# A retention layer and a rational FFN on one core: every engine in a hand-written order, two chunks landed in FFN buffers, weights joined in two VectorE steps

## The chip, the core and the metric

The kernel runs on one NeuronCore of a Trainium2 chip. The core has a matrix engine (TensorE, PE in the profile, with its weight loads as PEld), three engines for elementwise work (VectorE or DVE, ScalarE or ACT, GpSimd or POOL), and an engine that issues DMAs (SyncE or SP). Each takes its own instructions in the order in which they stand in its queue; semaphores make one wait for another. The metric is the device time of one execution in microseconds.

## The reference

A retention layer (a linear attention with a decaying state) feeds a feed-forward layer with a rational activation:

```python
for t in range(S):          # B, H, S, D = 4, 8, 768, 64
    state = gamma[None, :, None, None] * state + np.einsum('bhd,bhe->bhde', k[:, :, t], v[:, :, t])
    y[:, :, t] = scale * np.einsum('bhd,bhde->bhe', q[:, :, t], state)
...
h = x @ w_in                # x: 3072 tokens x 512, w_in: 512 x 2048
P = a[0] + a[1] * h + a[2] * h2 + a[3] * h3
Q = 1.0 + np.abs(b[0]) * np.abs(h) + np.abs(b[1]) * h2
g = P / (Q + 1e-06)
return (g @ w_out).astype(np.float32)   # w_out: 2048 x 512
```

The weights arrive as 64-bit floats and are made into 32-bit ones on the chip.

## The kernel before

**Attention.** The 3072 tokens are 24 chunks of 128, six to a batch element. A chunk has four tiles of 256 KB (`kT`, `qT`, `v`, `k`; the last chunk of a batch element needs no `k`). Its work comes in two parts. Part 0: POOL scales `v` and the state, PE makes the scores `pa` (16 small matmuls), VectorE multiplies them with the causal mask into `aT`. Part 1: PE adds into `px` what the state recalls (L213), the values (L221) and the new outer product of `k` and `v` (L233); VectorE scales the result, ScalarE rounds it to `xh`, VectorE takes the rest `xl`, and adds the outer product to the state.

**FFN.** Four chunks make a block of 512 tokens, six blocks `n`; the hidden layer is 16 tiles `f` of 128. One pair `(n, f)` is a slot: `gemm_in` (12 matmuls into `ph`: high and low parts of `x` and of the weights), then `poly` and `ratio` on ScalarE, VectorE and POOL, `split` of the result into `gh` and `gl`, and three slots later (`LAG`) `gemm_out`, 12 matmuls into the four accumulators `po`. `order` lists the 96 slots: blocks 0 and 1 with the first half of the hidden tiles, then both with the second half (slots 0 to 31, so that weights are needed half as fast), then blocks 2 to 5 whole. The halves of blocks 0 and 1 are parked in DRAM and added later.

**Weights.** Each of 32 weight tiles lands as `raw` (512 KB, pairs of 32-bit words). To decode one, ScalarE takes the magnitude of the high word into a PSUM bank `u`; VectorE shifts it (L106), joins the low word's top bits (L109) and the sign (L115) into `t`; ScalarE rounds `t` to the high half of `w` (L125), POOL takes the rest (L126).

**Memory.** Of PSUM's eight banks four hold `po` (and, before `po` exists, `u` and `px`), and four are one pool for `u`, `px`, `pa` and `ph`. Chunks have two buffers of each kind.

**Order.** Only SP's queue stands as the code has it. For the other four engines a scheduler with a timeline of its own decides the order; source order only sets which buffers are reused. Chunks 0 to 3 run ahead of slot 0, chunks 4 to 7 are placed in slots 0 to 7, chunks 8 to 11 in slots 24 to 31, and each later block's chunks in the 16 slots ahead of it.

Of the kernel before, what the change touches and what calls it, by code (L numbers as in the profile page):

```python
# [19 lines left out]
def tile_retention_rational_ffn(  # L20
# [31 lines left out]
    ps = ctx.enter_context(tc.tile_pool(name="ps", bufs=8 - SPB, space=PSUM))  # L52
# [4 lines left out]
    def bank(name, dtype=F32):  # L57

        if name in ("u", "px") and not o_tiles:
# [12 lines left out]
    qcon = const.tile([P, 1], F32, name="qcon")  # L72
    state = const.tile([P, NP, D], F32, name="state")
# [19 lines left out]
    def decode():  # L93

        ts = {}

        def magnitude(i):


            ts[i] = u = bank("u", U32)  # L100
            nc.scalar.activation(  # L101
                u.bitcast(F32), raws[i][:, :, 1].bitcast(F32), AF.Abs, scale=2.0 ** -112
            )

        def shift(i):
            nc.vector.tensor_scalar(ts[i], ts[i], 3, None, ALU.logical_shift_left)  # L106

        def low(i):
            nc.vector.scalar_tensor_tensor(  # L109
                ts[i], raws[i][:, :, 0], 29, ts[i], ALU.logical_shift_right, ALU.bitwise_or  # L110
            )

        def sign(i):
            t = ff.tile([P, DM], U32, name="t", bufs=TBUFS)
            nc.vector.scalar_tensor_tensor(  # L115
                t, raws[i][:, :, 1], 0x80000000, ts[i], ALU.bitwise_and, ALU.bitwise_or
            )
# [12 lines left out]
        for i in range(len(tiles)):  # L130
            if i + 1 < len(tiles):
                magnitude(i + 1)
            low(i)
            if i + 1 < len(tiles):
                shift(i + 1)
            sign(i)
            split_weight(i)
            done.add(tiles[i])
            yield

    decoding = decode()

    def need(m, f):
        while (m, f) not in done:
            next(decoding)
# [205 lines left out]
    def attend(k):  # L351
        for i, part in parts.get(k, ()):
# [7 lines left out]
            if k < 0:  # L360
                fetch()
# [109 lines left out]
```

## Time and profile before

| | |
|---|---|
| time, median of 3 runs | 664.7 us (664.12 to 664.72) |
| the profiled execution | 666.62 us, span of its instructions 664.8 us |
| granted TensorE clock, mean | 0.98 |
| PE idle before its last matmul | 31.5 us (span 664.8, busy 628.4, 4.9 behind the last matmul) |
| DMA landings, median | `raw` 6.3 and 7.0 us, `kT` 2.7 us, `v` 3.1 us |
| bytes moved | 52.36 MB, 43.33 MB read from HBM |

The page of the profile gives each engine's busy time, its share in 40 slices of the span, and groups of instructions of one line and shape with their mean time and with what ended the idle time before them (`<-` names it). A table of stretches gives busy times between two moments. In a timeline row stand start, length, engine, line, operation, what is written `<-` what is read, a count, and in brackets the idle time before and what ended it. PE's instructions are pipelined, so a busy PE can still be slow: how far it is from its best rate is seen from counts.

### The profile page before, as it was taken

Reading aid. Unit: us, or ns where it says so; the run is one execution under the profiler, and the core shown is the slowest. Engines: PE = TensorE matmul, PEld = TensorE weight load, DVE = VectorE, ACT = ScalarE, POOL = GpSimd, SP = SyncE. Lnnn points to the kernel's source line nnn. Section 1 sums busy time; section 2 is a strip of 40 time slices with the busy share of each in tenths; the row PEclk is TensorE's granted clock in tenths of the full one; section 3 lists DMA queues with packets and bytes.
Section 4 is the critical chain, followed back from the end, with each engine's and each line's share of the span. In section 5 each row is a group of like instructions: output and inputs, shape, how many; then the busy total and the mean of one; then the engine's idle time right before and its main releaser. Section 6 shows DMA issues by size and latency. Waiting matters only on the chain.

```text
span 664.8 us, 9995 instructions
## 1 busy us (share of the span) xinstructions
PE 628.4 (95%) x3712; PEld 508.6 (76%) x3712; DVE 457.4 (69%) x749; ACT 426.8 (64%) x715; POOL 323.9 (49%) x272
## 2 busy tenths in 40 slices
PE   4657999899999999999999999999999999999997
PEld 3545787688788778878888878888888888888885
DVE  4967879898876866684566657566656756766663
ACT  3436668898884555664676566666566566777773
POOL 3645457576654434443544434544444344454442
PEclk9677999999999999999999999999999999999999
DMA  8878434100102332340110222111221000010001
GB/s 306 325 230 347 160 115 170 64 0 1 64 1 80 111 128 80 103 120 17 48 49 0 65 87 74 33 24 41 65 80 33 1 0 1 12 52 1 0 1 63
DMA packets 24384, 52.36 MB, mean 79 GB/s; under 512 B 3088, under 2 KB 3216, under 8 KB 24336
## 3 DMA queue, kind: packets, MB, share of 16 engines
q1 hardware_dynamic: 24336, 51.73, 22.9%
q8 instruction: 29, 0.48, 0.3%
q14 instruction: 19, 0.16, 0.1%
HBM read 43.33 MB, written 8.39 MB: 78 GB/s over the span
## 4 chain that ended last, share of the span: by engine, by line
PE 86%; DVE 5%; DMA 3%; ACT 2%; issue 2%; POOL 1%; SPq 0%; ACTq 0%; POOLq 0%; DVEq 0%
PE po L305 39%; PE ph L259 37%; PE pa L197 4%; PE px L221 3%; PE px L213 2%; PE px L233 1%; DMA raw<-in_w_out 1%; DMA raw<-in_w_in 1%; POOL w L126 1%; DVE t L115 1%; DMA k<-in_k 1%; DVE u L109 1%; DVE ph L283 1%; DVE q L282 0%; ACT u L101 0%
## 5 line engine op out<-in xcount | busy, mean ns | idle before, releaser
L259 PE MATMUL ph<-xh,w 128*128 128x512 f32 x768 | 206.7, 393 | 4.2 <-ACT xh L243 2.2
L305 PE MATMUL po<-w,gh 128*128 128x512 f32 x768 | 201.8, 396 | 2.5 <-ACT t L322 2.5
L272 POOL TENSOR_TENSOR q<-q,s 128x512 f32<-128x512 f32 x96 | 124.2, 1294 | 144.6 <-ACT s L271 143.0
L291 POOL TENSOR_TENSOR gl<-p,gh 128x512 fp32r<-128x512 f32 x96 | 123.7, 1293 | 116.7 <-ACT gh L290 61.8
L259 PEld LDWEIGHTS ph<-xh,w 128*128 128x128 f32 x768 | 144.4, 189 | 36.5 <-DVE p L284 2.8
L305 PEld LDWEIGHTS po<-w,gh 128*128 128x128 f32 x768 | 141.0, 188 | 35.5 <-ACT t L322 3.3
L274 DVE TENSOR_TENSOR p<-ph,p 128x512 f32<-128x512 f32 x96 | 66.1, 689 | 103.2 <-ACT p L273 103.2
L305 PE MATMUL po<-w,gl 128*128 128x512 f32 x384 | 109.5, 390 | 0.0
L290 ACT CAST gh<-p 128x512 fp32r<-128x512 f32 x96 | 59.5, 620 | 69.8 <-DVE p L284 65.6
L282 DVE SCALAR_TENSOR_TENSOR q<-q,qcon,ph 128x512 f32<-128x512 f32 x96 | 71.4, 744 | 47.6 <-ACT ph L281 46.9
L259 PE MATMUL ph<-xl,w 128*128 128x512 f32 x384 | 104.2, 392 | 0.0
L270 ACT ACTIVATE q<-ph 128x512 f32<-128x512 f32 x96 | 57.2, 596 | 69.4 <-PE ph L259 68.9
L280 ACT ACTIVATE s<-q,qcon 128x512 f32<-128x512 f32 x96 | 69.6, 725 | 42.1 <-POOL q L272 41.3
L259 PEld LDWEIGHTS ph<-xl,w 128*128 128x128 f32 x384 | 72.6, 189 | 15.4
L305 PEld LDWEIGHTS po<-w,gl 128*128 128x128 f32 x384 | 72.0, 188 | 15.2
L271 ACT ACTIVATE s<-q,babs 128x512 f32<-128x512 f32 x96 | 78.0, 812 | 0.0
L273 ACT ACTIVATE p<-ph,par_sb 128x512 f32<-128x512 f32 x96 | 74.3, 774 | 0.0
L275 DVE SCALAR_TENSOR_TENSOR p<-p,par_sb,ph 128x512 f32<-128x512 f32 x96 | 71.4, 744 | 1.8
L283 DVE SCALAR_TENSOR_TENSOR ph<-p,par_sb,ph 128x512 f32<-128x512 f32 x96 | 72.0, 750 | 0.0
L284 DVE SCALAR_TENSOR_TENSOR p<-q,ph 128x512 f32<-128x512 f32 x96 | 64.7, 683 | 1.3
L281 ACT ACTIVATE ph<-s 128x512 f32<-128x512 f32 x96 | 57.9, 603 | 4.6 <-DVE p L275 2.3
L126 POOL TENSOR_TENSOR w<-t,w 128x512 fp32r<-128x512 f32 x32 | 41.1, 1286 | 23.6 <-ACT w L125 23.4
(31 smaller groups left out, 439.4 us busy)
## 6 DMA issues: line engine op xcount, KB each, us to landing
raw<-in_w_in SPq DMA_DIRECT2D x16, 512.0 KB, 6.3
raw<-in_w_out SPq DMA_DIRECT2D x16, 512.0 KB, 7.0
kT<-in_kT SPq DMA_DIRECT2D x24, 256.0 KB, 2.7
qT<-in_qT SPq DMA_DIRECT2D x24, 256.0 KB, 2.9
v<-in_v SPq DMA_DIRECT2D x24, 256.0 KB, 3.1
k<-in_k SPq DMA_DIRECT2D x20, 256.0 KB, 3.5
out<-t SPq DMA_DIRECT2D x16, 256.0 KB, 2.4
half<-t SPq DMA_DIRECT2D x8, 256.0 KB, 2.3
```

Of the source, the lines that this page charges most:

```text
L259: nc.tensor.matmul(ph, w1[f][:, part, kt * P : (kt + 1) * P], x[:, kt], start=(i == 0), stop=(i == 3 * NP - 1),)
L271: nc.scalar.activation(s, q, AF.Identity, bias=babs[:, 0:1], scale=babs[:, 1:2])
L272: nc.gpsimd.tensor_mul(q, q, s)
L273: nc.scalar.activation(p, ph, AF.Identity, bias=par_sb[:, 2:3], scale=par_sb[:, 3:4])
L274: nc.vector.tensor_mul(p, ph, p)
L275: nc.vector.scalar_tensor_tensor(p, p, par_sb[:, 1:2], ph, ALU.add, ALU.mult)
L280: nc.scalar.activation(s, q, AF.Abs_reciprocal_sqrt, bias=qcon[:, 0:1])
L282: nc.vector.scalar_tensor_tensor(q, q, qcon[:, 0:1], ph, ALU.add, ALU.mult)
L283: nc.vector.scalar_tensor_tensor(ph, p, par_sb[:, 0:1], ph, ALU.add, ALU.mult)
L284: nc.vector.scalar_tensor_tensor(p, q, 2.0, ph, ALU.subtract, ALU.mult, reverse0=True)
L291: nc.gpsimd.tensor_sub(gl, p, gh.bitcast(F32))
L305: nc.tensor.matmul(o_tiles[n][tt], g_[:, tt * P : (tt + 1) * P], w2[f][:, part], start=(first and m == 0), stop=(last and m == 2),)
```

## The change

Four things change together.

1. **Order.** All four compute engines are scheduled by hand: their instructions stand in source order. The old parts of attention and decode become small functions, and `opening()` and `run()` call them in an order written out. The opening goes chunk by chunk with one weight tile decoded in each; every slot decodes one more until all are done. Values come behind the outer product and the recall; `gh` of a slot is made in the next one.
2. **Landings.** `kT`, `qT`, `k` and `v` of chunks 2 and 3 land in buffers of the FFN (`gh`, `gl`, `q`) which are not yet in use, so that six chunks are loaded ahead.
3. **Decode.** ScalarE reads the fourth byte of each low word and writes its top three bits (scale 1/32, a bias, rounding) to `t`; VectorE's first step shifts the magnitude and joins these bits, the second joins the sign. The shift as a step of its own is gone. The weights are decoded four hidden tiles of `w_in` ahead instead of two, in two halves.
4. **FFN.** In the slots that decode but have no part of attention (8 to 23), the step `s` runs on POOL as a tensor_scalar instead of on ScalarE. `ph` gets two banks of its own, and `u`, `px`, `pa` share the other two. Copies of `po` alternate between ScalarE and VectorE, and parked halves are fetched a slot ahead.

```diff
-    ps = ctx.enter_context(tc.tile_pool(name="ps", bufs=8 - SPB, space=PSUM))
+    ps = ctx.enter_context(tc.tile_pool(name="ps", bufs=(8 - SPB) // 2, space=PSUM))
...
-        return ps.tile([P, TB], dtype, name=name, tag="bank")
+        return ps.tile([P, TB], dtype, name=name, tag="ph" if name == "ph" else "bank")
...
-        def shift(i):
-            nc.vector.tensor_scalar(ts[i], ts[i], 3, None, ALU.logical_shift_left)
-        def low(i):
-            nc.vector.scalar_tensor_tensor(
-                ts[i], raws[i][:, :, 0], 29, ts[i], ALU.logical_shift_right, ALU.bitwise_or
-            )
...
+    def decode_low(i):
...
+        ts[i] = ff.tile([P, DM], U32, name="t", bufs=3)
+        byte = raws[i].rearrange("p m w -> p (m w)").bitcast(U8)[:, 3::8]
+        nc.scalar.activation(ts[i], byte, AF.Identity, bias=lcon[:, 0:1], scale=1.0 / 32)
...
+    def decode_join(i):
...
+        nc.vector.scalar_tensor_tensor(
+            u, u, 3, ts[i], ALU.logical_shift_left, ALU.bitwise_or
+        )
+        nc.vector.scalar_tensor_tensor(
+            ts[i], raws[i][:, :, 1], 0x80000000, u, ALU.bitwise_and, ALU.bitwise_or
+        )
...
+    borrowed = {2: ("gh", "gh", "q", "gl"), 3: ("gh", "gl", "q", "gl")}
...
+    def opening():
+
+        scale_v(0)
+        scores(0)
+        for i in range(SPB):
+            mask(i)
+            outer(i)
+            recall(i)
+            values(i)
+            if i == 0:
+                decode_read(0)
+            update(i)
+            decode_join(i)
+            prepare(i + 1)
+            if i + 1 < SPB:
+                scores(i + 1)
+            x_out(i)
+            decode_split(i)
+            decode_rest(i)
+            decode_read(i + 1)
+        decode_join(SPB)
+        decode_read(SPB + 1)
...
+        if on_pool:
+            nc.gpsimd.tensor_scalar(
+                s, q, babs[:, 1:2], babs[:, 0:1], op0=ALU.mult, op1=ALU.add
+            )
+        else:
+            nc.scalar.activation(s, q, AF.Identity, bias=babs[:, 0:1], scale=babs[:, 1:2])
...
     def run():
...
+            plain = part is None and tile_ < len(tiles)
...
+                mid[k] = poly_scalar(gemm_in(*order[k]), plain)
...
+            if 0 < k <= nslot:
+                g[k - 1] = split(mid.pop(k - 1)[1])
...
+            if part == 1:
+                outer(chunk)
+                recall(chunk)
+                values(chunk)
             if k >= LAG:
                 n, f = order[k - LAG]
                 gemm_out(n, f, *g.pop(k - LAG))
...
+            if part == 0:
+                scores(chunk)
+                load_k_t(chunk + 2)
+            if plain:
+                decode_read(tile_ + 1)
+                decode_join(tile_)
+            if k < nslot:
+                ratio_scalar(*mid[k])
...
+            elif k < nslot:
+                ratio_vector(*mid[k])
```

The number of matmuls on PE doesn't change, nor that of the DMAs. Three places show what the new order does.

VectorE from its first step in the opening, before the change (L106, L109, L115 are the three steps of decode, L202 the mask, L242 and L244 the two halves of `x`, L247 the state):

```order
L106 TENSOR_SCALAR u<-u 128x512
L109 SCALAR_TENSOR_TENSOR u<-raw,u 128x512
L202 TENSOR_TENSOR aT<-pa,causal_sb 128x512
L115 SCALAR_TENSOR_TENSOR t<-raw,u 128x512
L202 TENSOR_TENSOR aT<-pa,causal_sb 128x512
L242 TENSOR_TENSOR px<-px,xdec_sb 128x256
L106 TENSOR_SCALAR u<-u 128x512
L244 TENSOR_TENSOR xl<-px,xh 128x2x128
L109 SCALAR_TENSOR_TENSOR u<-raw,u 128x512
L115 SCALAR_TENSOR_TENSOR t<-raw,u 128x512
L242 TENSOR_TENSOR px<-px,xdec_sb 128x256
L244 TENSOR_TENSOR xl<-px,xh 128x2x128
```

Chunk 0 stood between the steps of two weight tiles, and four more tiles were joined before chunk 2. Now its whole step reads so (L222 the mask, L269 the state, L126 and L129 the two joins, L281 and L286 the halves of `x`), and the next chunk's mask follows:

```order
L222 TENSOR_TENSOR aT<-pa,causal_sb 128x512 x2
L269 COPY state<-px 128x256
L126 SCALAR_TENSOR_TENSOR u<-u,t 128x512
L129 SCALAR_TENSOR_TENSOR t<-raw,u 128x512
L281 TENSOR_TENSOR px<-px,xdec_sb 128x256 x2
L286 TENSOR_TENSOR xl<-px,xh 128x2x128 x2
L222 TENSOR_TENSOR aT<-pa,causal_sb 128x512 x2
```

The state's update moved ahead of `x`, and one tile is decoded to a chunk.

PE where `gemm_out` sets in, before the change (L259 is `gemm_in`, L305 `gemm_out`, L197 scores, L221 values):

```order
L221 MATMUL px<-aT,v 64x128 x8
L259 MATMUL ph<-xh,w 128x512 x4
L259 MATMUL ph<-xl,w 128x512 x4
L259 MATMUL ph<-xh,w 128x512 x4
L197 MATMUL pa<-qT,kT 128x128 x4
L305 MATMUL po<-w,gh 128x512 x4
L305 MATMUL po<-w,gl 128x512 x2
L197 MATMUL pa<-qT,kT 128x128 x4
L305 MATMUL po<-w,gh 128x512 x2
L305 MATMUL po<-w,gl 128x512
```

And the same kind of place now, slots 4 and 5 (L325 `gemm_in`, L380 `gemm_out`, L213 scores, L234 outer product, L258 values):

```order
L380 MATMUL po<-w,gh 128x512 x8
L380 MATMUL po<-w,gl 128x512 x4
L213 MATMUL pa<-qT,kT 128x128 x8
L325 MATMUL ph<-xh,w 128x512 x4
L325 MATMUL ph<-xl,w 128x512 x4
L325 MATMUL ph<-xh,w 128x512 x4
L234 MATMUL px<-v,k 64x64 x8
L258 MATMUL px<-aT,v 64x128 x8
L380 MATMUL po<-w,gh 128x512 x8
L380 MATMUL po<-w,gl 128x512 x4
```

Scores stood in the middle of a `gemm_out`; now each kind of work stands in one piece, and each part of a chunk in a slot of its own.

ScalarE in a slot that decodes without attention, before the change (L270, L271 and L273 are abs, `s` and `p`, L280 and L281 rsqrt and square, L290 `gh`, L101 and L125 decode):

```order
L290 CAST gh<-p 128x512
L270 ACTIVATE q<-ph 128x512
L273 ACTIVATE p<-ph,par_sb 128x512
L280 ACTIVATE s<-q,qcon 128x512
L271 ACTIVATE s<-q,babs 128x512
L281 ACTIVATE ph<-s 128x512
L101 ACTIVATE u<-raw 128x512
L125 CAST w<-t 128x512
```

The rsqrt there belongs to the slot before. Now, in slot 9 (L336 and L344 abs and `p`, L364 `gh` of the slot before, L110 and L118 the two reads of decode, L353 and L354 rsqrt and square, L139 the rounding of `w`):

```order
L336 ACTIVATE q<-ph 128x512
L344 ACTIVATE p<-ph,par_sb 128x512
L364 CAST gh<-p 128x512
L110 ACTIVATE t<-raw,lcon 128x512
L118 ACTIVATE u<-raw 128x512
L353 ACTIVATE s<-q,qcon 128x512
L354 ACTIVATE ph<-s 128x512
L139 CAST w<-t 128x512
```

`s` is gone to POOL, a second read has come, and rsqrt and square of a slot stand in that slot, behind `gh` of the one before.

More of the change, by code (lines that the diff above doesn't have):

```diff
@@ L10 @@
 U32 = mybir.dt.uint32
+U8 = mybir.dt.uint8
 AF = mybir.ActivationFunctionType
@@ L57, in bank @@
     def bank(name, dtype=F32):
-        if name in ("u", "px") and not o_tiles:
+        if name in early:
             early[name] += 1
@@ L141, in tile_retention_rational_ffn, with decode_read, decode_high @@
[L141 to L145, printed above, removed]
+    us, ts = {}, {}
+    def decode_read(i):
+        decode_low(i)
+        decode_high(i)
+    def decode_low(i):
+        if i >= len(tiles):
+            return
+        ts[i] = ff.tile([P, DM], U32, name="t", bufs=3)
+        byte = raws[i].rearrange("p m w -> p (m w)").bitcast(U8)[:, 3::8]
+        nc.scalar.activation(ts[i], byte, AF.Identity, bias=lcon[:, 0:1], scale=1.0 / 32)
+    def decode_high(i):
+        if i >= len(tiles):
+            return
+        us[i] = bank("u", U32)
+        nc.scalar.activation(
+            us[i].bitcast(F32), raws[i][:, :, 1].bitcast(F32), AF.Abs, scale=2.0 ** -112
+        )
@@ new lines, in prepare, with scores @@
+    def prepare(i):
+        if i < NSTEP:
+            scale_state(i)
+            scale_v(i)
+    def scores(i):
+        st = steps[i]
+        pa = [bank("pa").rearrange("p (h t) -> p h t", t=P) for _ in range(2)]
+        for aj in range(NP):
+            for r in range(2):
+                rows = slice(r * D, (r + 1) * D)
+                nc.tensor.matmul(
+                    pa[r][:, aj], st["kT"][rows, aj], st["qT"][rows, aj], start=True, stop=True
+                )
+        st["pa"] = pa
@@ L194, in attention, with mask, outer @@
+    def mask(i):
+        st = steps[i]
+        for r in range(2):
+            st["aT", r] = at.tile([P, NP, P], F32, name="aT")
+            nc.vector.tensor_mul(
+                st["aT", r], st["pa"][r], causal_sb.unsqueeze(1).broadcast_to([P, NP, P])
+            )
+    def outer(i):
+        st = steps[i]
+        px = st["px"] = [bank("px") for _ in range(2)]
+        if i % C < C - 1:
+            pk = st["pk"] = px[1][:, TB // 2 :].rearrange("p (h d) -> p h d", d=D)
             for aj in range(NP):
@@ new lines, in values @@
+    def values(i):
+        st, c = steps[i], i % C
+        for r in range(2):
+            for a in range(2):
+                for j in range(2):
+                    nc.tensor.matmul(
+                        st["px"][r][j * D : (j + 1) * D, a * P : (a + 1) * P],
+                        st["v"][:, 4 * a + 2 * r + j],
+                        st["aT", r][:, 2 * a + j],
+                        start=(c == 0),
+                        stop=(c == 0 or a == 1), skip_group_check=True,
+                    )
@@ L338, in tile_retention_rational_ffn @@
     }
-    parts = {-1: [(i, part) for i in range(SPB) for part in range(2)]}
+    parts = {}
     for n in range(1, NB):
```

349 lines of the change are left out of this document (180 added, 169 removed).

## The prediction

> **What bounds the kernel now.** I read the busy times first, then the slices of the span, then a table of stretches of the instructions that touch a decoded weight tile `w`, and last the timeline of the opening. TensorE (PE) is the bound, and where it isn't busy the time is lost:
>
> ```profile
> PE 628.4 (95%) x3712; PEld 508.6 (76%) x3712; DVE 457.4 (69%) x749; ACT 426.8 (64%) x715; POOL 323.9 (49%) x272
> PE   4657999899999999999999999999999999999997
> PEclk9677999999999999999999999999999999999999
> ```
>
> After the fourth slice (16.6 us each) PE is nearly full. But "busy" doesn't say whether the stage moves at its best rate. The FFN has 2304 large matmuls (96 slots, 12 of `ph` and 12 of `po` each), and the best rate is in the chain, late in the kernel:
>
> ```profile
> 635.43 2.72 PE ph L259 x12
> ```
>
> 2.72 us for 12 is 0.2267 us each: 5.44 us a slot, 522 us in all. The stretches below are cut where slots 0, 7, 24, 48, 64 and 80 start and where the last matmul ends; PE's count in them is of large matmuls alone:
>
> ```profile
> core 0: us, PE busy (x) PEld busy (x) ACT busy (x) POOL busy (x), PEclk, DMA share, GB/s
> 0.00:43.02 43.02, 0.00 (x0) 0.00 (x0) 6.80 (x11) 12.96 (x11) 0.80 0.80 286
> 43.02:102.42 59.40, 41.12 (x156) 30.31 (x157) 3.72 (x6) 8.75 (x7) 0.94 0.63 220
> 102.42:195.28 92.86, 88.39 (x385) 71.70 (x384) 9.26 (x15) 19.41 (x15) 1.00 0.12 46
> 195.28:360.23 164.95, 137.21 (x577) 106.41 (x576) 0.00 (x0) 0.00 (x0) 1.00 0.24 74
> 360.23:462.08 101.85, 89.74 (x385) 71.38 (x384) 0.00 (x0) 0.00 (x0) 1.00 0.17 53
> 462.08:564.54 102.46, 89.76 (x385) 71.38 (x384) 0.00 (x0) 0.00 (x0) 1.00 0.09 29
> 564.54:659.90 95.36, 95.36 (x421) 78.64 (x419) 0.00 (x0) 0.00 (x0) 1.00 0.03 12
> ```
>
> So: 43.0 us pass before the first large matmul, and at 102.4 us, with all of chunks 0 to 7 of attention done, only 156 of the 2304 are through. The third stretch holds 384 (87.1 us at the best rate; a count one higher is one that straddles a cut) and takes 92.9: 5.8 lost. The next three hold 576 + 384 + 384 and 16 chunks; above the best rate they take 34.4 + 14.8 + 15.4 = 64.6 us, 4.0 a chunk, but 3.7 in the best of them. The last holds 420 at the best rate. Behind 659.9 lie 4.9 us of copies and stores.
>
> Why the first stretch is long shows in PE's timeline:
>
> ```profile
> 4.21 2.08 PE L197 MATMUL pa<-qT,kT 64*128 64x128 f32 x16 [4.21 <-DMA qT<-in_qT]
> ...
> 25.54 2.08 PE L197 MATMUL pa<-qT,kT 64*128 64x128 f32 x16 [3.55 <-DMA qT<-in_qT]
> ...
> 37.96 1.23 PE L213 MATMUL px<-qT,state 64*64 64x128 f32 x16 [6.56 <-POOL state L190]
> ...
> 60.36 2.07 PE L259 MATMUL ph<-xh,w 128*128 128x512 f32 x4
> 62.23 1.91 PE L259 MATMUL ph<-xl,w 128*128 128x512 f32 x4
> 63.94 1.74 PE L259 MATMUL ph<-xh,w 128*128 128x512 f32 x4
> ```
>
> Chunk 3's scores wait for a landing at 25.5, and its recall for the state until 38.0. VectorE had been joining weights that nobody needed yet (the order's first rows show it). The last three rows are one `ph` of 12 at 60.4: 5.25 us instead of 2.72.
>
> **The change, part by part.** These are the group rows for the steps that move, with mean ns and what they waited for:
>
> ```profile
> L290 ACT CAST gh<-p 128x512 fp32r<-128x512 f32 x96 | 59.5, 620 | 69.8 <-DVE p L284 65.6
> L280 ACT ACTIVATE s<-q,qcon 128x512 f32<-128x512 f32 x96 | 69.6, 725 | 42.1 <-POOL q L272 41.3
> L271 ACT ACTIVATE s<-q,babs 128x512 f32<-128x512 f32 x96 | 78.0, 812 | 0.0
> L281 ACT ACTIVATE ph<-s 128x512 f32<-128x512 f32 x96 | 57.9, 603 | 4.6 <-DVE p L275 2.3
> L282 DVE SCALAR_TENSOR_TENSOR q<-q,qcon,ph 128x512 f32<-128x512 f32 x96 | 71.4, 744 | 47.6 <-ACT ph L281 46.9
> L283 DVE SCALAR_TENSOR_TENSOR ph<-p,par_sb,ph 128x512 f32<-128x512 f32 x96 | 72.0, 750 | 0.0
> L284 DVE SCALAR_TENSOR_TENSOR p<-q,ph 128x512 f32<-128x512 f32 x96 | 64.7, 683 | 1.3
> L202 DVE TENSOR_TENSOR aT<-pa,causal_sb 128x512 f32<-128x512 f32 x48 | 31.6, 684 | 9.8 <-PE pa L197 9.8
> L106 DVE TENSOR_SCALAR u<-u 128x512 uint32<-128x512 uint32 x32 | 22.2, 695 | 13.5 <-ACT u L101 13.3
> L109 DVE SCALAR_TENSOR_TENSOR u<-raw,u 128x512 uint32<-128x512 uint32 x32 | 22.1, 692 | 0.4
> L101 ACT ACTIVATE u<-raw 128x512 f32<-128x512 f32 x32 | 20.4, 637 | 12.5 <-DMA raw<-in_w_in 8.0 <-DMA raw<-in_w_out 3.2 <-DVE t L115 1.0
> L242 DVE TENSOR_TENSOR px<-px,xdec_sb 128x256 f32<-128x256 f32 x48 | 20.3, 426 | 8.6 <-PE px L221 8.2 <-PE px L233 0.3
> L272 POOL TENSOR_TENSOR q<-q,s 128x512 f32<-128x512 f32 x96 | 124.2, 1294 | 144.6 <-ACT s L271 143.0
> ```
>
> *Opening (landings, decode, order).* In the new order VectorE does in each of the four steps: two masks (1.37 us), the state's update (0.42, as one of the 256-wide rows), two joins (1.38), two 256-wide products and two subtractions (4 x 0.43 = 1.7). That is 4.9 us, with no wait but for PE's values, which the update and joins cover, and for ScalarE's `xh` between products and subtractions. The bound from landings: chunks 0 to 3 (four 256 KB tiles each), the four `raw` tiles of 512 KB queued through chunk 3 and 0.33 MB of constants are 6.6 MB, 23 us at the table's 286 GB/s; reading tile 3 (two ScalarE steps), joining it and making chunk 3's `x` is about 4 us more. From the first scores' end (4.21 + 2.08 = 6.3) four steps of 5 us give 26.3. I take **27 us** for the first large matmul, where it was 43.0; ends 25 and 33 (a landing lost at each of chunks 2 and 3, priced near the 3.55 wait). On SP's queue the loads of chunks 4 and 5 now stand ahead of the later `raw` tiles and wait for the buffers of chunks 0 and 1; these come free in the first two steps, by 17 us, while what is queued ahead of them takes 23 us to land, so nobody waits for that.
>
> *Slots 0 to 7.* The same 156 matmuls and chunks 4 to 7 took 59.4 us before, which would end at 86.4. Step by step: the first `ph` runs like the one at 60.4, 5.25 us, until 32; slot 0 then runs abs, s, p, two products, mask, read, two joins and three ratio steps to 41; slots 1 and 2 add 6 and 8 (mask and join sit in front of the even slots' ratio, and ScalarE's read waits for the mask to free a bank, with the next slot's abs queued behind it; PE's second `ph` bank covers that); at 55 PE has done four `ph`, one `po` and six chunks. Left are 8 x 2.72 and two chunks at 3.7, 29.2 us: 84.2, and a stall of 1. I take **85 us** where 102.4 stood: **17.4 gained**. VectorE's sum over eight slots (five ratio and poly steps 3.6, a join pair 1.4, mask or `x` 1.9: 6.9, or 55 in all) gives 82; each slot paying 1.5 us of handovers more gives 95.
>
> The Trainium skill's "TensorE: Matmul & The Clock Gate", Part 1, has PE drop to half rate after an idle window of about 3.4 us and stay there for as long. The rows at 60.4 agree: 5.25 for 2.72, after an idle stretch. By that rule alone slots 1 and 2 could be cold too, 5 us on PE and, with nothing to cover it, 90 for 85; I count one.
>
> *Slots 8 to 23 (a tile decoded in each).* The third join step goes: 32 x 0.695 = 22 us less on VectorE. ScalarE gets a read of one byte per weight; its price is not in the trace. The nearest rows are the plain read at 637 (which strides over words as well) and the activation with a bias tile at 812: I take 0.70, ends 0.60 and 0.81. Sixteen of the `s` steps move from ScalarE to POOL: 812 ns go, and a POOL step comes that the trace doesn't have; nearest is L272's 1294 (two inputs, one operation), which I take, with ends 1.04 and 2.59 (twice that row, for two operations). POOL then has four steps of 1.29, 5.2 of 5.44 us.
>
> The Trainium skill's "GPSIMD Engine Reference" (§3 and §4.1) speaks against this move: elementwise work belongs on VectorE. It gives one-input work some 1.8 cycles an element, 769 ns for 512, which no row here shows; by that the POOL step would be an estimated 0.8 us and the sum below the same, since POOL isn't last.
>
> What is last is a loop through ScalarE and VectorE: `gh` of the slot before, the two reads, rsqrt, square, three ratio steps, which release the next `gh`: 0.62 + 0.70 + 0.64 + 0.73 + 0.60 + 0.74 + 0.75 + 0.68 = 5.46. Four neighbours of it don't depend on each other and overlap by 0.1, as the first pair of rows here does (0.60 long, next start 0.49 later); some five handovers add about 0.2:
>
> ```profile
> 605.55 0.60 ACT L270 ACTIVATE q<-ph 128x512 f32<-128x512 f32 x1 [0.70 <-PE ph L259]
> ...
> 606.04 0.78 ACT L273 ACTIVATE p<-ph,par_sb 128x512 f32<-128x512 f32 x1
> ...
> 611.84 0.69 DVE L284 SCALAR_TENSOR_TENSOR p<-q,ph 128x512 f32<-128x512 f32 x1
> ```
>
> So 5.3 against 5.44: PE sets the pace, barely. Copies of `po` halves are shared by two engines and come a slot ahead of need. I put **2.0 lost** for the 5.8 of before (ends 0.5 and 16): **3.8 gained**.
>
> *Two banks for `ph`.* `ph` of slot k+2 waits for the ratio of slot k. From the start of abs, right behind `ph`, to the end of the ratio the three rows above show 611.84 + 0.69 - 605.55 = 7.0; PE has 3 x 2.72 = 8.16 us to do in between, more with attention. No cost; without that cover it costs half the excess in every slot.
>
> *Chunks 8 to 23.* PE's rows alternate in whole blocks instead of single matmuls. I take 3.6 each, 58 us for 64.6: **6.6 gained**; ends 55 and 65. The tail keeps its 4.9.
>
> Sum: 17.4 + 3.8 + 6.6 = 27.8. The profiled execution has a span of 664.8 in a time of 666.6; the median of the runs is 664.7, and I subtract from that: **637 us**.
>
> **Rivals.**
> - *The loop or POOL paces slots 8 to 23.* With the POOL step at 2.59, POOL needs 6.5 a slot, 16 us in sixteen; with the loop at 6.0, 9 us: 645 to 653. For it: ScalarE's and VectorE's sums are within 0.2 of PE's. Against: L272's idle, 144.6 us.
> - *The first tensor_scalar on POOL comes late.* POOL has run only products and subtractions. A delay of d at slot 8 costs d less the 1.2 of slack, once. "GPSIMD Engine Reference", §2.1, gives some 6 us for a first call into freshly loaded code. From rows alone the price lies between 0 and a slot, 5.4: up to 642. Against: the order shows no extra load.
> - *Chunks 2 and 3 don't land sooner.* Then the opening keeps its waits of 3.55 and 6.56: 27 becomes 37, 647.
> - *Slower: the fixed order makes a chain of every slot.* Before, a scheduler filled each wait; now each engine stops at the first wait in its queue, and two `ph` banks give PE two slots of cover. Where the chain from `ph` to ratio is longer than 8.8 us, PE loses over 0.33 in each of 88 slots, 29 us, and the kernel ends above 666. Against: the late rows show 7.0, and the new order puts `s` ahead of `p`.
> - *Better:* slot 7 ends at 82, nothing lost to 23, chunks at 3.5: 630.
>
> **How the numbers follow.** Forecast 0.55; the loop or POOL 0.17; better 0.10; late landings 0.08; late first call 0.05; slower chain 0.05. The range 630 to 650 holds the forecast, the late call and landings, most of the better case and half of the paced one: above eight in ten. A run can tell about 0.2% (1.3 us) from no change. Faster 0.94, same 0.01, slower 0.05.
>
> **What would show it.** First `ph` near 27 us and the `ph` that follows 60 `po` near 85; slots 8 to 23 at 5.44 with POOL's `s` at 1.0 to 1.3; a chunk at 3.6 to 3.7 with no wait of PE on a ratio. A first `ph` after 33, a wait of PE's `ph` on the last ratio step in most slots, or a POOL step over 1.6 makes the prediction wrong.

## The result, and the profile after

| | before | after |
|---|---|---|
| time, median of 4 runs | 664.71 us (664.12 to 664.97) | 648.58 us (647.85 to 649.76) |
| ratio | | 0.976 (95%: 0.9743 to 0.9777) |
| span of the profiled execution | 664.8 us | 648.0 us |

The forecast was 637 us in a range of 630 to 650. Sign and range hold, but 16.1 us were gained where 27.8 were forecast. The three lines of the page that were read first, after the change:

```profile
PE 623.6 (96%) x3712; PEld 503.8 (78%) x3712; DVE 460.5 (71%) x730; ACT 441.7 (68%) x721; POOL 333.6 (51%) x288
PE   5777999999999999999999999999999999999997
PEclk9877999999999999999999999999999999999999
```

PE is full from the fifth slice on, as before, but slices 2 to 4 stand at 7. The table of stretches, cut at the same slots as before (0, 8, 24, 48, 64, 80, and the last matmul's end), of instructions that touch a decoded `w`:

```profile
0.00:34.51 34.51, 0.00 (x0) 0.00 (x0) 1.86 (x3) 3.86 (x3) 0.89 0.97 359
34.51:97.99 63.48, 42.99 (x156) 31.86 (x156) 6.59 (x11) 13.53 (x11) 0.87 0.57 195
97.99:185.62 87.63, 87.63 (x385) 72.05 (x385) 9.69 (x16) 20.04 (x16) 1.00 0.15 56
185.62:346.08 160.46, 135.91 (x577) 106.74 (x576) 1.22 (x2) 3.90 (x3) 1.00 0.25 76
346.08:446.88 100.80, 89.41 (x385) 71.46 (x384) 0.00 (x0) 0.00 (x0) 1.00 0.17 53
446.88:548.42 101.54, 89.40 (x385) 71.46 (x384) 0.00 (x0) 0.00 (x0) 1.00 0.09 29
548.42:644.27 95.85, 95.67 (x421) 78.56 (x419) 0.00 (x0) 0.00 (x0) 1.00 0.04 14
```

The columns are those of the table before: stretch and length, then busy time and count of PE, PEld, ACT and POOL, the granted clock, DMA share and GB/s. Term by term, with 0.2267 us for a large matmul as the best rate:

| | before | forecast | after | gained (forecast) |
|---|---|---|---|---|
| first `ph` | 43.0 | 27 | 34.5 | 8.5 (16.0) |
| slots 0 to 7 | 59.4 | 58 | 63.5 | -4.1 (1.4) |
| lost in slots 8 to 23 | 5.8 | 2.0 | 87.63 - 87.06 = 0.6 | 5.2 (3.8) |
| chunks 8 to 23 | 64.6 | 58 | 29.9 + 13.7 + 14.5 = 58.1 | 6.5 (6.6) |
| slots 80 to 95 over the best rate | 0.1 | 0.1 | 0.6 | -0.5 (0) |
| behind the last matmul | 4.9 | 4.9 | 3.7 | 1.2 (0) |

The gains add up to 16.8, the difference of the two spans. Everything from slot 8 on came out within 1.5 us of its term or better. The first 98 us brought 4.4 of the 17.4 us that they were to bring.

**Where the opening's time went.** PE's timeline, chunks 2 and 3 (L213 scores, L234 outer product, L247 recall, L258 values):

```profile
21.98 0.69 PE L234 MATMUL px<-v,k 128*64 128x64 f32 x16 [1.81 <-DMA qT<-in_qT]
22.60 0.67 PE L247 MATMUL px<-qT,state 64*64 64x128 f32 x16
23.19 1.86 PE L258 MATMUL px<-aT,v 128*64 128x128 f32 x16
24.98 2.00 PE L213 MATMUL pa<-qT,kT 64*128 64x128 f32 x16
28.77 0.69 PE L234 MATMUL px<-v,k 128*64 128x64 f32 x16 [1.79 <-DVE xl L286]
```

And VectorE's in the same step (L271 update, L126 and L129 joins, L281 products, L286 subtractions, L222 masks):

```profile
25.16 0.42 DVE L271 TENSOR_TENSOR state<-px,state 128x256 f32<-128x256 f32 x1 [2.24 <-PE px L258]
25.50 0.69 DVE L126 SCALAR_TENSOR_TENSOR u<-u,t 128x512 uint32<-128x512 uint32 x1
26.23 0.69 DVE L129 SCALAR_TENSOR_TENSOR t<-raw,u 128x512 uint32<-128x512 uint32 x1
26.83 0.76 DVE L281 TENSOR_TENSOR px<-px,xdec_sb 128x256 f32<-128x256 f32 x2
27.75 0.76 DVE L286 TENSOR_TENSOR xl<-px,xh 128x256 fp32r<-128x256 f32 x2 [0.16 <-ACT xh L282]
28.42 1.28 DVE L222 TENSOR_TENSOR aT<-pa,causal_sb 128x512 f32<-128x512 f32 x2
```

One step is a closed loop. From outer product to outer product it takes 28.77 - 21.98 = 6.79 us: 1.21 until the values start (23.19), 1.97 until the update starts (25.16), 0.34 + 1.33 for update and joins (26.83), 0.92 for products and rounding (27.75), 1.02 until `xl` has left the two `px` banks (28.77). (In the row at 21.98 the profile names a landing of `qT`, which the outer product doesn't read; `xl` left the banks at 20.97 + 0.76 = 21.73, and the outer products of chunks 1 and 3 come as shortly behind their `xl`.) VectorE's part of the loop is 6.79 - 2.24 = 4.55, with 0.16 of waiting for `xh` in it, under the forecast's 4.9; the rest is 2.24 of waiting at the update. The update reads only the outer product, finished by 22.7, but that lies in the same tile as part of the values, and the profile has the update start when the *values* end. Behind it in VectorE's queue stand two joins that need neither. The forecast had the joins cover the wait for the values; they stand behind the instruction that waits.

**Where slots 0 to 7 lost 5.5 us.** PE's rows in slots 0, 2 and 3 (L325 `gemm_in`, L380 `gemm_out`):

```profile
34.52 2.07 PE L325 MATMUL ph<-xh,w 128*128 128x512 f32 x4 [2.72 <-ACT xh L282]
...
49.27 1.20 PE L325 MATMUL ph<-xh,w 128*128 128x512 f32 x4 [2.74 <-DVE p L359]
50.30 1.59 PE L325 MATMUL ph<-xl,w 128*128 128x512 f32 x4
51.69 1.91 PE L325 MATMUL ph<-xh,w 128*128 128x512 f32 x4
...
60.17 0.40 PE L247 MATMUL px<-qT,state 64*64 64x128 f32 x2 [2.25 <-DVE aT L222]
62.29 1.12 PE L247 MATMUL px<-qT,state 64*64 64x128 f32 x14 [1.71 <-DVE t L129]
63.34 1.97 PE L258 MATMUL px<-aT,v 128*64 128x128 f32 x16
65.25 1.22 PE L380 MATMUL po<-w,gh 128*128 128x512 f32 x2
```

In slot 3 PE has done its fourth `ph` by 57.9 and then stands at the recall of chunk 5, first for the mask, then for a bank that `u` of a weight tile holds until the join L129 ends (62.2). Queued behind it is the first `gemm_out`, whose `gl` had been ready since 51.3. Slot 4 starts at 69.26, 34.7 us after slot 0, where the forecast's steps put it 28 after; slots 4 to 7 then take 28.7, forecast 30.

### The profile page after: what moved, and what is told of

Read it like the earlier page. It is cut to its first block, busy times and chain, and to the rows that moved or that the text cites. A ratio compares the mean times of both kernels' runs of the same rounds, so it can differ in the third digit from the quotient of the medians.

```text
span 648.0 us, 9942 instructions
## 1 busy us (share of the span) xinstructions
PE 623.6 (96%) x3712; PEld 503.8 (78%) x3712; DVE 460.5 (71%) x730; ACT 441.7 (68%) x721; POOL 333.6 (51%) x288
## 4 chain that ended last, share of the span: by engine, by line
PE 88%; ACT 3%; DVE 3%; DMA 3%; issue 1%; SPq 1%; POOLq 0%; DVEq 0%; ACTq 0%
PE ph L325 40%; PE po L380 39%; PE px L258 3%; PE pa L213 3%; PE px L247 2%; PE px L234 2%; DMA qT<-in_qT 1%; DMA k<-in_k 1%; DMA xdec_sb<-in_xdec 1%; ACT s L342 1%; DVE u L126 1%; ACT q L336 0%; SPq L174 0%; DVE t L129 0%; DVE p L348 0%
## 5 line engine op out<-in xcount | busy, mean ns | idle before, releaser
L325 PE MATMUL ph<-xh,w 128*128 128x512 f32 x768 | 211.2, 397 | 5.8 <-DVE p L359 2.9
L380 PE MATMUL po<-w,gh 128*128 128x512 f32 x768 | 201.0, 394 | 0.0
L325 PEld LDWEIGHTS ph<-xh,w 128*128 128x128 f32 x768 | 143.8, 190 | 39.4 <-ACT xh L282 4.1
L380 PEld LDWEIGHTS po<-w,gh 128*128 128x128 f32 x768 | 143.3, 189 | 32.7 <-ACT p L344 1.9
L336 ACT ACTIVATE q<-ph 128x512 f32<-128x512 f32 x96 | 57.2, 596 | 126.4 <-PE ph L325 126.3
L380 PE MATMUL po<-w,gl 128*128 128x512 f32 x384 | 110.9, 390 | 0.2 <-POOL gl L365 0.2
L325 PE MATMUL ph<-xl,w 128*128 128x512 f32 x384 | 104.2, 394 | 0.0
L357 DVE SCALAR_TENSOR_TENSOR q<-q,qcon,ph 128x512 f32<-128x512 f32 x96 | 71.4, 744 | 39.3 <-ACT ph L354 39.2
L325 PEld LDWEIGHTS ph<-xl,w 128*128 128x128 f32 x384 | 72.8, 190 | 15.8
L380 PEld LDWEIGHTS po<-w,gl 128*128 128x128 f32 x384 | 72.4, 188 | 15.6 <-POOL gl L365 0.6
L353 ACT ACTIVATE s<-q,qcon 128x512 f32<-128x512 f32 x96 | 69.3, 722 | 15.3 <-POOL q L343 15.3
L344 ACT ACTIVATE p<-ph,par_sb 128x512 f32<-128x512 f32 x96 | 73.1, 761 | 0.0
L364 ACT CAST gh<-p 128x512 fp32r<-128x512 f32 x96 | 58.8, 612 | 15.1 <-DVE p L359 15.1
L342 ACT ACTIVATE s<-q,babs 128x512 f32<-128x512 f32 x80 | 65.3, 817 | 2.7
L354 ACT ACTIVATE ph<-s 128x512 f32<-128x512 f32 x96 | 57.8, 602 | 10.2 <-DVE p L349 0.4
```

The costliest lines, as they stand in the source:

```text
L325: nc.tensor.matmul(ph, w1[f][:, part, kt * P : (kt + 1) * P], x[:, kt], start=(i == 0), stop=(i == 3 * NP - 1),)
L342: nc.scalar.activation(s, q, AF.Identity, bias=babs[:, 0:1], scale=babs[:, 1:2])
L344: nc.scalar.activation(p, ph, AF.Identity, bias=par_sb[:, 2:3], scale=par_sb[:, 3:4])
L353: nc.scalar.activation(s, q, AF.Abs_reciprocal_sqrt, bias=qcon[:, 0:1])
L357: nc.vector.scalar_tensor_tensor(q, q, qcon[:, 0:1], ph, ALU.add, ALU.mult)
L380: nc.tensor.matmul(o_tiles[n][tt], g_[:, tt * P : (tt + 1) * P], w2[f][:, part], start=(first and m == 0), stop=(last and m == 2),)
```

## The experiments

"After" is the changed kernel at 648.58 us; each experiment was timed beside the kernel before. Times are medians of four runs (of six for e10); the last two columns, and the stretches in the text, are from one profiled execution each.

| | edit | us | ratio to before (95%) | first `ph` | slot 8 starts |
|---|---|---|---|---|---|
| after | | 648.6 | 0.976 (0.9743 to 0.9777) | 34.5 | 98.0 |
| e1 | joins ahead of the update | 640.9 | 0.9654 (0.9629 to 0.968) | 28.8 | 89.0 |
| e2 | `px` of chunks 0 and 2 in other banks | 644.1 | 0.9697 (0.9683 to 0.9712) | 30.4 | 91.8 |
| e3 | e1 and e2 | 640.8 | 0.9639 (0.9618 to 0.966) | 27.9 | 89.3 |
| e4 | slot 3: output ahead of recall | 646.7 | 0.9727 (0.9695 to 0.976) | 33.6 | 93.8 |
| e9 | e1 and e4 | 636.6 | 0.9582 (0.9566 to 0.9598) | 26.8 | 84.8 |
| e5 | no landings in FFN buffers | 647.9 | 0.9742 (0.9724 to 0.9759) | 35.0 | 98.6 |
| e11 | e1, e4, e5 | 636.6 | 0.958 (0.9564 to 0.9595) | 26.5 | 84.4 |
| e6 | decode in three VectorE steps | 658.8 | 0.9906 (0.989 to 0.9922) | 38.7 | 103.8 |
| e7 | `s` on ScalarE everywhere | 651.7 | 0.9801 (0.9777 to 0.9826) | 34.4 | 96.1 |
| e8 | the scheduler orders the new source | 700.6 | 1.0533 (1.0515 to 1.0551) | 39.9 | 99.6 |
| e10 | extra matmuls in the opening | 652.7 | 0.9849 (0.9813 to 0.9886) | 39.0 | 99.9 |
| e12 | e1, e4, e10 | 648.5 | 0.9757 (0.9742 to 0.9772) | 39.0 | 96.8 |

**e1: the joins ahead of the update.** In `opening()`:

```diff
-            update(i)
             decode_join(i)
+            update(i)
```

> In the changed kernel the opening takes 6.8 us a chunk (masks at 21.64 and 28.42), where 5.0 was forecast, and VectorE stands 2.2 to 3.3 us idle in each step in front of the state's update, which waits for PE's values although it reads only the outer product; the joins that were to cover the values are queued behind it. Here the joins of the opening stand ahead of the update, nothing else. Theory A (the queue order holds the step): joins run while PE makes the values; each of chunks 1 to 3 gets 1.3 us shorter, chunk 0, whose weight tile lands late, 0.7; first large matmul at 34.5 - 4.6 = 30 us, time 648.6 - 4.6 = 644. Rival B (outer products that wait for the banks freed by x hold the step): step stays within 0.3 of 6.8, time within 1 us of 648.6.

640.85 us, 7.7 less than after, more than the expected 4.6. Exchanging two lines brings nearly half of what the whole change brought (16.1). The first `ph` comes at 28.8 instead of 34.5 and, behind shorter waits, runs at PE's full rate.

**e2: other banks for `px`.** The `px` tiles of chunks 0 and 2 are taken from the two `ph` banks, which are free in the opening, so that an outer product doesn't wait until the chunk before has left its banks:

```diff
-        px = st["px"] = [bank("px") for _ in range(2)]
+        px = st["px"] = [
+            ps.tile([P, TB], F32, name="px", tag="ph") if i in (0, 2) else bank("px")
+            for _ in range(2)
+        ]
```

> In the changed kernel all chunks of the opening make px in the same two banks, so PE's outer product of a chunk starts only when the x of the chunk before has left them (14.17 after 13.92, 21.98 after 21.73, 28.77 after 28.51), in front of recall and values. Here chunks 0 and 2 of the opening make px in the two banks of ph, which are not in use before slot 0; order unchanged. Theory B (banks hold the step): outer product and recall run under the mask, values start right behind its first half, 1.4 us sooner in each of chunks 1 to 3: first large matmul at 30 to 31 us, time 648.6 - 4 = 644.5. Rival A (only the queue order on VectorE holds it): under 1 us gained, time 647.6 to 649.

644.1 us, 4.5 less than after. So the other link of the loop, `xl` to outer product, was a cost as well: breaking either link opens the loop.

**e3: both.**

> Both edits of the opening: joins ahead of the state's update, and px of chunks 0 and 2 in the banks of ph. If queue order and banks each hold the step, the gains add to the step that was forecast: 4.8 to 5.0 us a chunk, first large matmul at 27 to 28 us, and the time 648.6 - 7 = 641.5. If they hide one another (values end when the joins do, either way), about what the better of the two gives alone: 644. If landings set the pace behind them, first large matmul stays above 30 with PE or POOL waiting for DMA.

640.75 us, the same as e1 within the intervals; it is near the expected 641.5, but e1 alone gives that. Once the joins are out of the loop the second pair of banks moves the first `ph` by 0.9 us more, and slot 8 not at all (89.3 and 89.0). The 0.9 are still there in slot 3, where the recall of chunk 5 goes on at 53.35 (54.21 in e1), and are lost behind it: the first `gemm_out` takes 4.2 us in e3 and 3.2 in e1, at a lower rate of PE.

**e4: in slot 3 the output ahead of the recall.** In `run()`, for the one slot `k == LAG`:

```diff
-            if part == 1:
+            if part == 1 and k != LAG:
                 outer(chunk)
...
                 gemm_out(n, f, *g.pop(k - LAG))
...
+            if part == 1 and k == LAG:
+                outer(chunk)
+                recall(chunk)
+                values(chunk)
```

> In slot 3 of the changed kernel PE stands from 57.9 to 62.3 in front of chunk 5's recall, which waits for the mask until 60.2 and then for the bank that the decode of a weight tile holds until 62.2; the first gemm_out, whose gl was ready at 51.3, is queued behind it. Here gemm_out of slot 3 stands ahead of recall and values in that slot alone. Theory: PE fills the wait with 2.7 us of gemm_out, recall and values start at 62.3 as before, the next gemm_in at 65.3 instead of 69.3; time 648.6 - 4 = 644.6. Rival: slots 4 to 7 are paced by VectorE's chain anyway and take it back: time within 1 us of 648.6.

646.73 us, 1.9 less by the medians, where 4 were expected; the runs reach from 643.2 to 647.9. In its profile slots 0 to 7 take 60.2 us instead of 63.5, so 3.3 of the 4 are there. Its opening has the same code as after, yet not the same rows. The values of chunks 1 to 3 in e4:

```profile
15.93 1.09 PE L258 MATMUL px<-aT,v 128*64 128x128 f32 x16
...
21.96 1.09 PE L258 MATMUL px<-aT,v 128*64 128x128 f32 x16
...
28.89 1.97 PE L258 MATMUL px<-aT,v 128*64 128x128 f32 x16
```

After has 1.97, 1.86 and 1.82 there. PE's rate in a stretch of short waits differs from one execution to another, so this single experiment doesn't separate the order in slot 3 from the rate. The rows also price the rate in the opening: the step of e4 in which the values (at 21.96) run at the full rate takes 26.77 - 20.75 = 6.02 us, from outer product to outer product, where after's takes 6.79. So about 0.8 of that step is PE's lower rate; what remains above e9's 4.69 (below) is the order.

**e9: e1 and e4 together.**

> Joins ahead of the state's update in the opening, and gemm_out of slot 3 ahead of recall and values. Joins alone gave 640.85, gemm_out alone 646.73. They act in different places (before the first large matmul, and in slot 3), so if nothing behind takes it back they add: 648.6 - 7.7 - 1.9 = 639, slot 8 starting near 85 to 86 as the prediction had it. Rival: in the joins kernel PE also stood in slot 3 (46.9 to 60.2 us for slots 3 and its recall), so gemm_out ahead gains 3 us there: 637.5 to 638.5. If slots 4 to 7 are paced by VectorE, 640.5.

636.64 us (636.5 to 638.06), below all that was expected: with e11 the best version, 4.2% below the kernel before and 1.8% below the change (636.64 / 648.58). The edits bring 11.9 us together where they brought 7.7 and 1.9 alone. Beside e1's profile (639.0 us) e9's (634.9) is 4.1 shorter: 2.2 in slots 0 to 7 (60.2 in e1, 58.0 here), which is the second edit, and 1.9 ahead of the first `ph`, where both have the same code but e1 still had the values of chunk 1 at 1.98 us. By these two profiles about 10 of the 11.9 are the two edits and the rest PE's rate in the opening. PE's rows of a step in the opening, and the first `ph`:

```profile
18.45 0.69 PE L234 MATMUL px<-v,k 128*64 128x64 f32 x16 [1.38 <-POOL v L192]
...
23.14 0.69 PE L234 MATMUL px<-v,k 128*64 128x64 f32 x16 [1.29 <-POOL v L192]
23.76 0.67 PE L247 MATMUL px<-qT,state 64*64 64x128 f32 x16
24.35 1.09 PE L258 MATMUL px<-aT,v 128*64 128x128 f32 x16
26.84 1.29 PE L325 MATMUL ph<-xh,w 128*128 128x512 f32 x4 [1.39 <-ACT xh L282]
```

and the two first stretches that follow, cut at its slots 0, 8 and 24:

```profile
26.83:84.80 57.97, 40.60 (x156) 30.23 (x156) 6.59 (x11) 13.59 (x11) 0.94 0.75 268
84.80:172.52 87.72, 87.69 (x385) 72.04 (x385) 9.70 (x16) 20.04 (x16) 1.00 0.15 56
```

A step takes 23.14 - 18.45 = 4.69 us, VectorE's own work: it waits 0.16 in the step. The first `ph` at 26.8, slots 0 to 7 in 58.0, slot 8 at 84.8: these are the forecast's 27, 58 and 85. Its numbers were right for a program in which the two queues were ordered as its reasoning took them to be. Inside the 58 some luck remains: the forecast has slot 0's `ph` slow and a stall of 1, while in e9 slot 0 runs at the full rate and slot 2 waits 3.00 and takes 5.4.

**e5 and e11: the landings.** The chunks 2 and 3 land in their own two buffers, as before the change:

```diff
-    borrowed = {2: ("gh", "gh", "q", "gl"), 3: ("gh", "gl", "q", "gl")}
+    borrowed = {}
```

> Undoes one part of the change: chunks 2 and 3 land in the chunks' own two buffers, so their loads wait until chunks 0 and 1 have been read. Theory: the step of 6.8 us in the opening is set by VectorE's queue and px's banks, and landings have slack behind it (v of chunk 3 would be issued when chunk 1's values end, 18.3 us, and land by 22, while it is scaled at 26.2): first large matmul within 1 us of 34.5, time 647.5 to 650. Rival, as the prediction had it: each of chunks 2 and 3 loses a landing of some 3.5 us, first large matmul near 40, time 652 to 656.

> The kernel with joins ahead of the update and gemm_out of slot 3 first, but chunks 2 and 3 landing in the chunks' own buffers. With the slow step of the changed kernel this cost nothing (647.93 for 648.58). Theory: with steps of 4.7 us landings become late: v of chunk 3 is issued when chunk 1's values end (18 us), lands by 21.5 to 22, is scaled at about 23; the cover is 1 us, and raw tiles 4 and 5 land later by 4: 0 to 2 us more than with the borrowed buffers. Rival: first large matmul 4 us or more later, the time 4 more.

647.9 us against 648.6, and with e1 and e4 636.61 against 636.64: the landings in FFN buffers are worth nothing that can be measured, with long steps and with short ones. Without the borrowed buffers the loads do start later, but still early enough: `v` of chunk 3 is issued at 18.5 in e5 instead of 13.3, and POOL takes it up at 25.7; in e11 it is issued at 15.6 and taken up at 21.6.

**e6: the decode in three VectorE steps again.** ScalarE's byte read falls away, VectorE gets its shift back; order and all else as after:

```diff
-        decode_low(i)
+        if i < len(tiles):
+            ts[i] = ff.tile([P, DM], U32, name="t", bufs=3)
...
+        nc.vector.tensor_scalar(u, u, 3, None, ALU.logical_shift_left)
...
-            u, u, 3, ts[i], ALU.logical_shift_left, ALU.bitwise_or
+            u, raws[i][:, :, 0], 29, u, ALU.logical_shift_right, ALU.bitwise_or
```

> Undoes the decode alone: the low bits are joined from the low word by VectorE, in three steps a tile (shift, low, sign), and ScalarE's read of a byte (765 ns) goes. Theory: VectorE gets 0.65 us more in each step of the opening and in each of 16 decoding slots, where it has about 0.5 us of slack of 5.44; the loop through gh, read, rsqrt and ratio gets shorter by the read. Opening and slots 0 to 3 4 to 6 us longer, slots 8 to 23 0.2 longer each: time 652 to 657. Rival (the read on ScalarE costs what the shift on VectorE did): 647.5 to 650.

658.76 us, 10.2 more than after and above the expected 652 to 657. In its profile, which is 8.8 longer, the first `ph` is 4.2 later, slots 0 to 7 take 1.7 more, slots 8 to 23 2.4 more. The largest part of its price is paid in the opening, where VectorE stands in the loop, and a smaller one in slots 8 to 23, under which the forecast had listed it.

**e7: `s` on ScalarE in slots 8 to 23 too.**

```diff
-                mid[k] = poly_scalar(gemm_in(*order[k]), plain)
+                mid[k] = poly_scalar(gemm_in(*order[k]), False)
```

> Undoes the move of s alone: in slots 8 to 23 s runs on ScalarE (817 ns) instead of POOL (771 ns). Theory: ScalarE's sum in such a slot, now 4.8 us from start to start, becomes 5.5 and passes PE's 5.44; its order puts s ahead of gh, so the loop of ScalarE and VectorE is delayed with it: 0.1 to 0.3 us a slot once the cover is used up, time 650 to 653. Rival (ScalarE has room, and PE keeps the pace): within 1 us of 648.6.

651.69 us, 3.1 more; slots 8 to 23 lose 3.8 instead of 0.6. Two neighbouring slots in VectorE's timeline of e7 (L357 starts the ratio):

```profile
150.29 0.75 DVE L357 SCALAR_TENSOR_TENSOR q<-q,qcon,ph 128x512 f32<-128x512 f32 x1 [0.25 <-ACT ph L354]
...
155.82 0.75 DVE L357 SCALAR_TENSOR_TENSOR q<-q,qcon,ph 128x512 f32<-128x512 f32 x1 [0.25 <-ACT ph L354]
```

5.53 us a slot, each time waiting for ScalarE: with `s` there the loop through ScalarE is slower than PE's 5.44 and sets the pace. After, the same step of VectorE comes every 5.37 us in such slots, and a slot takes 87.63 / 16 = 5.48 in the mean. But 0.09 a slot is only some 1.4 of the 3.8. The greater part, 2.7, is lost around the two places where `po` is copied out, in slots of 6.11, 5.85, 5.75 and of 6.45 and 5.74: a loop at 5.37 can make up for the copies, one at 5.53 can't.

**e8: the new source, ordered by the scheduler.** Buffers, banks and decode as after; only the block that fixes the four engines to source order is left away:

```diff
-        with tc.manual_schedule(engines=COMPUTE):
-            opening()
-            run()
+        opening()
+        run()
```

> Undoes the hand-made order alone: the new source with its landings, decode and banks, but the four compute engines ordered by the scheduler as before. Theory: the 6.5 us in chunks 8 to 23 and the 5.2 us in slots 8 to 23 that the change gained come from the order (work in whole blocks, copies of po shared and in time) and go again, while the opening is not slower: time 655 to 662. Rival (those gains come from the banks and the shared copies, not from the order): within 3 us of 648.6. Should the scheduler use the waits of the opening better than the hand-made order, the first large matmul comes before 34.5.

700.58 us, far above every expectation and 5.3% slower than before. PE's rows for one chunk part in e8 (`...` leaves out later parts):

```profile
394.58 1.52 PE L380 MATMUL po<-w,gh 128*128 128x512 f32 x6
396.03 0.71 PE L213 MATMUL pa<-qT,kT 64*128 64x128 f32 x4
396.67 0.50 PE L380 MATMUL po<-w,gh 128*128 128x512 f32 x1
...
398.26 0.71 PE L213 MATMUL pa<-qT,kT 64*128 64x128 f32 x4
398.90 0.44 PE L247 MATMUL px<-qT,state 64*64 64x128 f32 x4
```

and one part in after:

```profile
402.09 1.16 PE L213 MATMUL pa<-qT,kT 64*128 64x128 f32 x16
403.18 1.19 PE L325 MATMUL ph<-xh,w 128*128 128x512 f32 x4
```

A block of 16 takes 403.18 - 402.09 = 1.09 us, four of them alone 396.67 - 396.03 = 0.64: each of the two pieces shown costs about 0.37 more than its quarter of the block (0.64 - 0.27). PE is "busy" all along, and its total rises from 623.6 to 666.9 us. Slots 48 to 63 of e8:

```profile
377.09:490.86 113.77, 94.78 (x384) 70.10 (x385) 0.00 (x0) 0.00 (x0) 1.00 0.15 47
```

That is 26.7 above the best rate, where after has 13.7. In slots 8 to 23 e8 loses 20.4, 9.2 of it in waits of `ph` for the last ratio step and more in a chunk that the scheduler drew forward. So without the fixed order the other edits don't bring the gain. But the scheduler breaks the new source into more pieces than the old one, so e8 doesn't measure what whole blocks gained. That is read from the scores in 270 to 590 us of the two profiles, before and after:

```profile
L197 PE MATMUL pa<-qT,kT 64*128 64x128 f32 x176 | 16.2, 285 | 0.0
L213 PE MATMUL pa<-qT,kT 64*128 64x128 f32 x176 | 12.8, 285 | 0.0
```

These are 11 chunks: 3.4 us less, 0.31 a chunk, or an estimated 4.9 of the 6.5 us that 16 chunks gained.

**e10 and e12: matmuls that keep PE busy.** In each step of the opening 20 more small matmuls (40 by the profile's count) go into an otherwise free `ph` bank; they add nothing to the output.

```diff
+    def warm(i):
+        ph = ps.tile([P, TB], F32, name="warm", tag="ph")
+        for a in range(20):
+            nc.tensor.matmul(
+                ph[:, :P], steps[i]["kT"][:D, 0], steps[i]["qT"][:D, 0], start=True, stop=True
+            )
...
+            warm(min(i + 1, SPB - 1))
```

> The changed kernel with 20 more small matmuls behind the scores of each step of the opening, on chunk data, into an unused bank that nobody reads; they add no result. The joins kernel gained 7.7 where 4.6 was expected, and its values took 1.09 us from chunk 2 on, against 1.97, 1.86 and 1.82 here. Theory (PE runs at half rate when it idles in each step, and that lengthens the chain): with PE kept busy over the gap in front of the outer product, values take 1.1 us, each step of chunks 2 and 3 gets 1 to 1.8 shorter, the first large matmul comes at 30 to 32, its ph takes 2.8 instead of 5, time 643 to 645.5. Rival (the rate doesn't matter, or the added matmuls stand in the way): 648 to 650.

> The kernel with joins ahead of the update and gemm_out of slot 3 first, with the 20 added matmuls a step as well (no result in them). Theory: there PE is at full rate from chunk 2 on anyway, so only chunk 1 gains, 1 us, and the added matmuls stand in the way of nothing: 0 to 1 us less than without them. Rival: with the shorter step there is no gap to fill, they delay outer product and recall by their 1.2 us a step: 2 to 4 us more.

652.7 us (651.4 to 658.7), 4.1 more than after, and 648.5, 11.9 more than e9: both are slower than the theory and the rival had it. PE's rows in e12:

```profile
19.80 4.63 PE L221 MATMUL warm<-qT,kT 64*128 64x128 f32 x40
24.35 0.69 PE L241 MATMUL px<-v,k 128*64 128x64 f32 x16
24.97 0.67 PE L254 MATMUL px<-qT,state 64*64 64x128 f32 x16
25.57 1.09 PE L265 MATMUL px<-aT,v 128*64 128x128 f32 x16
...
34.38 4.73 PE L221 MATMUL warm<-qT,kT 64*128 64x128 f32 x40
39.04 1.21 PE L333 MATMUL ph<-xh,w 128*128 128x512 f32 x4
```

The filler did what it was to do: PE has no pause from 12 us to the first `ph`, and everything behind the filler runs at the full rate (values 1.09, `ph` 1.21). But 40 of them take 4.6 us a step, more than the pauses that they fill, and the first `ph` is 12.2 us later than in e9, which is the whole difference. In e10 the first `ph` is 4.5 us later than in after, and slots 0 to 7 take 61.0 instead of 63.5. These runs show that a PE without pauses runs the opening at full rate; the dose was far too high to tell whether a smaller one pays, so the theory that the lower rate costs time is not tested by them.

## Why the prediction came out as it did

- **Opening, 27 forecast, 34.5 measured: wrong.** The failed step is "4.9 us, with no wait but for PE's values, which the update and joins cover". The update itself waits for the values, and the joins are queued behind it; a step took 6.8. e1 shows it: with the two exchanged 5.7 of the 7.5 us come back. e2 shows the loop's second link, which the forecast didn't have. The landings, by which the forecast came to 27 as well, didn't bind: the first stretch moved 359 GB/s where 286 was taken. By the prediction's own sign, a first `ph` after 33, its account of the opening is refuted, though the time lies in the range.
- **Slots 0 to 7, 58 forecast, 63.5 measured: wrong.** The forecast let VectorE's chain end and did not ask what PE's queue holds behind the recall of chunk 5. It had the first `ph` cold and a stall of 1; measured were waits of 2.74 in slot 2 and 2.25 + 1.71 in slot 3. e4 alone recovers 3.3 in its profile; with e1 the stretch takes the 58.0 that was forecast.
- **The clock.** Two of the first three slots have a cold `ph` (one at a lower rate), 0 and 2, where I counted one. The `ph` at 49.27 has 1.59 and 1.91 for what takes 1.08, behind a wait of 2.74; from 51 to 55 us the granted clock is 0.61. The Trainium skill's "TensorE: Matmul & The Clock Gate", Part 1, has the clock fall after an idle window of about 3.4 us, and this window run freely, so that the number of slow matmuls varies from run to run. The traces agree with the variation (values of 1.97 in after and 1.09 in e4 from the same code); as to the 3.4 us, a pause of 2.74 was enough in after, while in e3 slot 2 comes behind one of 3.01 and runs at the full rate (1.20, 1.07 and 1.07, granted clock 1.00). The 90 for slot 8 that was worked out by that rule is nearer to 98.0 than my 85, though the greater part of the miss was waiting.
- **Slots 8 to 23, 2.0 lost forecast, 0.6 measured: right in mechanism, with two prices off.** The loop in these slots runs at 5.37 (5.3 forecast), just under PE's 5.44. The byte read took 0.77 (0.70 taken, ends 0.60 and 0.81). POOL's `s` took 0.77, where I took 1.29 with 1.04 as the lower end:

```profile
L338 POOL TENSOR_SCALAR s<-q,babs 128x512 f32<-128x512 f32 x16 | 12.3, 771 | 13.9 <-ACT q L336 13.9
L110 ACT ACTIVATE t<-raw,lcon 128x512 uint32<-128x512 uint8 x33 | 25.2, 765 | 6.3 <-DMA raw<-in_w_in 6.3
```

  The estimate by the Trainium skill's "GPSIMD Engine Reference" (§3.1: 769 ns for 512 elements in the best case) agrees with 771. Its advice, elementwise work on VectorE, was not tried by a run; e7, with the step on ScalarE, is 3.1 us slower.
- **The rivals.** The loop as the pace-setter didn't come, but was near: in e7, with `s` on ScalarE, it is 0.09 over PE's slot. The late first tensor_scalar didn't come: the 16 wait 13.9 us in all, 1.7 at most, for their input. That chunks 2 and 3 land no sooner was priced at 10 us; e5 and e11 give 0, since even the later loads of the chunks' own buffers are there in time. That this rival's 647 lies near 648.6 is chance. The slower fixed chain didn't come: it is the *scheduler* on the new source that is slower (e8).
- **Chunks 8 to 23, 58 forecast, 58.1 measured: right**, and for the reason given, whole blocks on PE: the scores alone make some 4.9 of the 6.5, and e8 shows what more pieces cost.
- **Tail, 4.9 forecast, 3.7 measured.** I kept it; the copies that ScalarE and VectorE now share are the likely cause, which no run tests.

That the time lay in the range is luck: the first two stages, which were to bring 17.4 us, brought 4.4. It lay there because the misses (7.5 and 5.5) were partly met by 1.4 and 1.2 more than forecast elsewhere, and because the range reached up to 650 for the sake of other rivals (a paced loop, late landings) than what came.

## What to carry to other kernels

In a fixed order ask of every instruction that waits what stands behind it in its queue and needs nothing of it: two such places, a state update ahead of two joins and a recall ahead of an output, were worth about 10 us, where the whole change had brought 16.1. Look where a tile that is read shares a bank with other work: here an update of one half of a `px` bank started only when the matmuls into the other half had ended (which rule makes it wait, no run separates). Small matmuls are kept in whole blocks, and an edit's price is measured in the stage in which its engine is the last, which for the decode was more the opening (4.2 us in e6) than slots 8 to 23 (2.4), where half the tiles are decoded.

## What the runs showed of the hardware that had not been expected

- Breaking a block of small matmuls costs PE time that the profile counts as busy: 0.64 us for 4 scores alone against 1.09 for 16 in one block; a kernel's PE total went from 623.6 to 666.9 us by order alone.
- PE's rate in a stretch of short waits isn't a property of the program: the same opening had its values at 1.97, 1.86 and 1.82 us in one execution and at 1.09, 1.09 and 1.97 in another. Nor does the length of the pause settle it: `ph` ran slow behind 2.74 us in after and 3.00 in e9, and at the full rate behind 2.69 in e4 and 3.01 in e3. Whether this also makes the spread of the runs (4.7 us in e4, 1.6 in e9) isn't shown.
